# Layer 2 of a routed kernel: rows gathered by quarters in groups of four, transposed in blocks by VectorE, with four output buffers

## The chip, the cores and the metric

The kernel runs on one core of a Trainium2 chip. The metric is the device time of one execution in microseconds (us); three runs of the kernel before gave 972.41, 974.34 and 975.12, median 974.34. In the profile PE is TensorE (PEld its weight loads), DVE is VectorE, ACT is ScalarE, POOL is GpSimd, SP is the queue that issues plain DMAs. Indirect DMAs (gathers and scatters of rows) are issued by POOL, in program order with its other work.

## The reference

An attention layer is followed by two mixture-of-experts layers of 8 experts over 2304 rows of 512 numbers. Layer 1 picks one expert per row, layer 2 two. The part that matters here is layer 2:

```
logits = x @ w_gate; noisy = logits + log1p(exp(x @ w_noise)) * noise
top2 = two largest of noisy per row; top2_w = softmax over these two
for e in range(8):
    for k in range(2):
        mask = top2[:, k] == e
        h = max(x[mask] @ w1[e], 0)            # 512 -> 1024
        out[mask] += top2_w[mask, k] * (h @ w2[e])   # 1024 -> 512
```

All of it is float32. The kernel splits each factor of a product into a high and a low part and adds three products, high·high, low·high and high·low.

## The kernel before

Attention and the routing of layer 1 are laid out by a planner with costs and due times (`Tasks.order`); layers 1 and 2 are written in the order in which they are issued (`full`, `pair`, `layer2`). Each engine runs its own instructions in that order.

At the end of each unit of layer 1, `x1_out` (L881) writes 2 × 128 finished rows to a DRAM buffer `xd` (520 numbers per row: 512 of data and 8 of noise). Rows of it that no unit writes are cleared during attention by DMAs on SP's queue, spread by the planner over the attention chunks (`M.later`, five DMAs to a chunk).

Layer 2 takes the 8 experts one after the other, 640 row slots (5 tiles of 128) each. The first two tiles of expert 0 are layer 1's last ones and are worked off while the routing of the last rows runs (`route2`); `slot_tables` then turns the routing into row numbers for the gathers (`l2g`) and the scatters (`l2s`). In the loop over experts e there are two stages:

- First products: `mm1` for 8 blocks f, in two halves of 304 columns each, 12 matmuls a half (L721 to L723) into a PSUM bank; ACT takes the high part (`hh`, L724), DVE the low part (`hl`, L726). There are two such banks. ACT and DVE also split the weights w2 (`split_w`, L696 and L697).
- Second products: `mm2` for 5 tiles, each in two half-tiles q of 12 matmuls of 512 columns (L731 to L733). Between half-tiles a list `todo` is worked off, with the splits of the next expert's w1 (`split_w1`, L700 and L701) and its 5 row tiles (`xsplit`): four transposes of 128×128 on TensorE against an identity (L711), then ACT's high part from PSUM (L712) and DVE's low part (L713). After each tile `l2_out` scales it on ACT into one of two output buffers (`os`, L973) and POOL scatters it with an addition into the output (L974). A scatter waits until the one before has landed.

The five gathers for expert e+1 (`l2_gather`, L704: 128 rows of 520 numbers each) are issued in one burst at the start of expert e, on POOL behind the scatters of expert e−1. If an expert has more than 640 rows, `overflow` does the rest; with these inputs it does not run.

Of the kernel before, what the change touches and what calls it, by code (L numbers as in the profile page):

```python
# [307 lines left out]
class Moe:  # L308
    def __init__(s, ctx, tc, ident, consts, areas):
# [3 lines left out]
        s.dram=ctx.enter_context(tc.tile_pool(name='dram',bufs=1,space=bass.MemoryType.DRAM))  # L313
        s.xd=s.dram.tile([N+SLOTS,XW],FT,name='xd')
# [35 lines left out]
    def blocks(s, nc, c, areas):  # L350
# [7 lines left out]
        s.w1r=V(T(K0,0,4096,'w1r'),KD); s.w2r=V(T(K0,4096,4096,'w2r'),KF); s.os=cut(K0,8192,512,'os',2)  # L358
# [6 lines left out]
        s.wb1=[V(T(HL,o,2048,'wb1%d'%o),2) for o in (2048,7168)]; s.wb2=V(T(W2,4096,4096,'wb2'),KF)  # L365
        s.x1=V(T(X1,0,2*XW,'x1'),2); s.ol2=V(T(OL,0,512,'ol2',FR),4); s.gs=cut(G,0,XW,'gs',GB); s.gn_=s.on_=0
# [603 lines left out]
    def l2_out(s, wk, y, tb, c, out):  # L970
# [3 lines left out]
        nc.gpsimd.indirect_dma_start(out=out,out_offset=bass.IndirectOffsetOnAxis(ap=si[:,c:c+1],axis=0),in_=o,in_offset=None,compute_op=OP.add)  # L974
    def l2_gather(s, wk, tb, c, ts=range(T2)):
        return [s.gather(s.xd[:],tb[0][:,c+t:c+t+1]) for t in ts]
    def layer2(s, w1, w2, out):
# [33 lines left out]
        V.tensor_copy(ov[:,NOV:],ue[:,E-1:E])  # L1011
        for e in range(E):
            nxt=e+1<E
            if nxt:
                if e: s.load_w(s.w1r,w1,E+e+1)
                g=s.l2_gather(wk,tb,(e+1)*TS)
            for f in range(KF):
# [4 lines left out]
                else: s.mm1(ps,f,EARLY,C2-EARLY)  # L1022
            if nxt and e: s.load_w(s.w2r,w2,E+e+1)
            ts=range(T2) if e else range(NE,T2)
            todo=[(lambda f=f:s.split_w1(f,nc.vector)) for f in range(KF)]
            for t in range(T2): todo.insert(2*t+1,lambda t=t:s.xsplit(ps,g[t],t*128))
            n=-(-len(todo)//(2*len(ts)-1))
            for t in ts:
                for q in range(2):
                    y=s.mm2(ps,t*128,range(4*q,4*q+4),y if q else None)  # L1030
                    if nxt:
                        for _ in range(n):
                            if todo: todo.pop(0)()
                s.l2_out(wk,y,tb,e*TS+t,out)
# [54 lines left out]
def build(tc, q, k, v, mz, beta, ids, mbias, wg, w1, w2, wcat, noise, out):  # L1089
    nc = tc.nc  # L1090
    with ExitStack() as ctx:
# [24 lines left out]
        M.later = [Q.add(100 * (5 + j // 5), SP, 1000, f, [A.sunk[4 + j // 5]]) for j, f in enumerate(dma)]  # L1116
# [51 lines left out]
```

## Time and profile before

| | us |
|---|---|
| median of 3 runs | 974.34 (972.41 to 975.12) |
| the profiled execution | 980.08 |
| its span, first to last instruction | 978.4 |
| TensorE busy | 941.9 (96%) |
| VectorE, ScalarE, GpSimd busy | 554.9, 487.9, 349.1 |
| mean granted clock of TensorE | 0.989 |

The page gives busy time by engine, the span in slices, the chain that ended last and the costliest groups of instructions. Attention fills the span up to about 190 us, layer 1 up to about 500, layer 2 the rest. Busy time of TensorE rests on modelled ends of matmuls, so lengths below are taken from start to start where that is possible.

### The profile page before, as it was taken

The numbers are of one execution on the slowest core, as the hardware profiler recorded it, in microseconds if no ns is written. First come the engines' busy times: TensorE is split into PE (matmuls) and PEld (weight loads), VectorE is DVE, ScalarE is ACT, GpSimd is POOL, SyncE is SP. The second block draws the span as 40 slices with busy tenths as digits, with TensorE's granted clock in tenths as the row PEclk, the third lists the DMA queues.
The fourth block names the chain that finished last, engine by engine and source line by source line (L and its number), as shares of the span: only waits on it lengthen the run. The fifth ranks groups of instructions, "written<-read, shape, count | busy, mean of one in ns | idle before, by whom it ended". The sixth has DMA issues, their size and how long they took to land. (4 is left out here: it accounts for less than half of the span.)

```text
span 978.4 us, 18585 instructions
## 1 busy us (share of the span) xinstructions
PE 941.9 (96%) x6849; PEld 828.6 (85%) x6849; DVE 554.9 (57%) x1697; ACT 487.9 (50%) x1141; POOL 349.1 (36%) x418
## 2 busy tenths in 40 slices
PE   7999999998999999999998999999999999999994
PEld 5888888878876888888887998898989889898983
DVE  8777777788765777777774344242443424253310
ACT  6887878775433565555552344333343434343320
POOL 5222231234552667776765130312213030221111
PEclk9999999999999999999999999999999999999997
DMA  8345856261595665555655163545346364435112
GB/s 212 102 111 178 268 193 207 78 225 59 192 313 188 214 215 195 191 193 202 216 198 159 38 172 97 128 132 129 77 113 168 97 137 130 122 78 119 22 23 35
DMA packets 83857, 144.98 MB, mean 148 GB/s; under 512 B 14497, under 2 KB 32929, under 8 KB 83745
## 3 DMA queue, kind: packets, MB, share of 16 engines
q1 hardware_dynamic: 73184, 117.10, 36.4%
q0 software_dynamic: 10560, 26.47, 13.6%
q8 instruction: 60, 0.98, 0.4%
q14 instruction: 53, 0.43, 0.1%
HBM read 111.65 MB, written 31.97 MB: 147 GB/s over the span
## 5 line engine op out<-in xcount | busy, mean ns | idle before, releaser
L721 PE MATMUL b<-xh,w1h 128*128 128x304 f32 (+3 forms) x800 | 240.5, 301 | 4.2 <-DVE hl L726 1.4
L722 PE MATMUL b<-xl,w1h 128*128 128x304 f32 (+3 forms) x800 | 237.7, 297 | 0.6 <-DVEq L791 0.3
L723 PE MATMUL b<-xh,w1l 128*128 128x304 f32 (+3 forms) x800 | 237.0, 296 | 0.0
L726 DVE SCALAR_TENSOR_TENSOR hl<-b,hh 128x304 fp32r<-128x304 f32 (+3 forms) x200 | 91.1, 455 | 209.3 <-ACT hh L724 198.1
L731 PE MATMUL b<-w2h,hh 128*128 128x512 f32 x464 | 187.8, 405 | 0.0
L974 POOL DMA_INDIRECT out_dram<-os,l2s x40 | 62.8, 1571 | 333.6 <-ACT os L973 256.9
L733 PE MATMUL b<-w2h,hl 128*128 128x512 f32 x464 | 181.6, 391 | 0.0
L732 PE MATMUL b<-w2l,hh 128*128 128x512 f32 x464 | 181.0, 390 | 0.0
L724 ACT ACTIVATE hh<-b 128x304 fp32r<-128x304 f32 (+3 forms) x200 | 81.8, 409 | 172.8 <-PE b L723 166.8
L721 PEld LDWEIGHTS b<-xh,w1h 128*128 128x128 f32 x800 | 152.6, 191 | 11.5 <-DVE hl L726 6.2
L722 PEld LDWEIGHTS b<-xl,w1h 128*128 128x128 f32 x800 | 152.6, 191 | 1.6 <-DVEq L791 0.5
L723 PEld LDWEIGHTS b<-xh,w1l 128*128 128x128 f32 x800 | 152.5, 191 | 0.0
L733 PEld LDWEIGHTS b<-w2h,hl 128*128 128x128 f32 x464 | 87.1, 188 | 19.4
L732 PEld LDWEIGHTS b<-w2l,hh 128*128 128x128 f32 x464 | 87.5, 188 | 15.5
L731 PEld LDWEIGHTS b<-w2h,hh 128*128 128x128 f32 x464 | 87.2, 188 | 15.4
L151 ACT ACTIVATE p<-sm,l 128x128 f32<-128x128 f32 (+4 forms) x144 | 84.1, 592 | 17.5 <-DVE l L147 17.5
L701 DVE TENSOR_TENSOR w1l<-w1r,w1h 128x512 fp32r<-128x512 f32 x86 | 71.5, 841 | 18.6 <-ACT w1h L700 18.3
L713 DVE TENSOR_TENSOR xl<-b,xh 128x512 fp32r<-128x512 f32 x56 | 38.6, 689 | 71.3 <-ACT xh L712 71.2
L696 ACT CAST w2h<-w2r 128x512 fp32r<-128x512 f32 x128 | 78.5, 613 | 0.0
L712 ACT CAST xh<-b 128x512 fp32r<-128x512 f32 x56 | 32.9, 587 | 87.4 <-PE b L711 87.4
L700 ACT CAST w1h<-w1r 128x512 fp32r<-128x512 f32 x128 | 74.8, 620 | 0.0
L973 ACT ACTIVATE os<-b,l2w 128x512 f32<-128x512 f32 x40 | 27.7, 691 | 94.1 <-PE b L733 47.9
(460 smaller groups left out, 1504.7 us busy)
## 6 DMA issues: line engine op xcount, KB each, us to landing
w1r<-in_w_dram SPq DMA_DIRECT2D x18, 2048.0 KB, 9.0
w2r<-in_w_dram SPq DMA_DIRECT2D x18, 2048.0 KB, 9.1
xd<-gs SPq DMA_DIRECT2D x24, 260.0 KB, 4.1
xd<-x SPq DMA_DIRECT2D x10, 520.0 KB, 10.8
out_dram<-gs SPq DMA_DIRECT2D x19, 256.0 KB, 3.8
k<-in_k_dram SPq DMA_DIRECT2D x16, 256.0 KB, 4.9
q<-in_q_dram SPq DMA_DIRECT2D x16, 256.0 KB, 3.3
v<-in_v_dram SPq DMA_DIRECT2D x16, 256.0 KB, 3.9
```

The lines of the kernel that those rows point to most:

```text
L151: s.nc.scalar.activation(s.P[b,i,u][:,lh*n:lh*n+n],s.SM[b,i,u][:,lh*n:lh*n+n],AF.Exp,scale=-1.0,bias=L[:,0,c:c+1],accum_out=L[:,1,c:c+1])
L696: nc.scalar.copy(hi[c],raw[:,c])
L700: nc.scalar.copy(s.w1h[:,:,fs],s.w1r[:,:,fs])
L701: eng.tensor_sub(s.w1l[:,:,fs],s.w1r[:,:,fs],s.w1h[:,:,fs].bitcast(FT))
L721: nc.tensor.matmul(h[:,:n],s.w1h[:,k,fs],s.xh[:,k,cs],start=k==0,stop=False)
L722: nc.tensor.matmul(h[:,:n],s.w1h[:,k,fs],s.xl[:,k,cs],start=False,stop=False)
L723: nc.tensor.matmul(h[:,:n],s.w1l[:,k,fs],s.xh[:,k,cs],start=False,stop=k==KD-1)
L724: def mm1_a(s, h, f, c0, n): s.nc.scalar.activation(s.hh[:,f,c0:c0+n],h[:,:n],AF.Relu)
L726: cs=slice(c0,c0+n); s.nc.vector.scalar_tensor_tensor(s.hl[:,f,cs],h[:,:n],0.0,s.hh[:,f,cs].bitcast(FT),op0=OP.max,op1=OP.subtract)
L731: nc.tensor.matmul(y,s.hh[:,f,cs],s.w2h[f],start=f==0,stop=False)
L732: nc.tensor.matmul(y,s.hh[:,f,cs],s.w2l[f],start=False,stop=False)
L733: nc.tensor.matmul(y,s.hl[:,f,cs],s.w2h[f],start=False,stop=f==KF-1)
```

## The change

Each unit's rows are written twice, to `xd` and, without the noise, to a second buffer `xq` in which every row is four rows of 128 numbers. Clearing covers `xq` too, with seven DMAs to a chunk. In layer 2's loop a tile is fetched by four gathers of 128 rows of 128 numbers: gather i brings, for slots 32i to 32i+31, quarter g of the row into partitions 32g to 32g+31 (`quarter_gather`, with the row numbers `gq4` from `quarter_tables`, made by four small products with a selection matrix from `quarter_sel`). One VectorE instruction then transposes the tile in blocks of 32×32 (`bsplit`), which puts feature 4P+j into partition P; w1 is loaded in the same order of features (`by='(p c)'`). ACT and DVE split from SBUF. Tiles 3 and 4 of expert 1 are gathered as whole rows and transposed on TensorE, by every fourth column (`xsplit` with `fourth`). The groups are spread over the loop by a table `plan`: tiles 1, 2 and 3 of the next expert after f = 1, 4 and 7 of the first products, tile 4 and tile 0 of the one after it between second products. Ahead of most groups GpSimd copies one column of a tensor that VectorE writes (`pace`), which holds the group back until then. The output buffers become four.

```diff
+        s.xq=s.dram.tile([4*SLOTS,D//4],FT,name='xq')
...
+        s.gq=cut(G,0,D,'gq',GB); s.xt_=[V(t,KD) for t in cut(X1,0,D,'xtq',2)]; s.xn=0; s.sel4=V(T(K1,8192,512,'sel4',FR),4); s.sel4f=V(T(K1,8704,512,'sel4f'),4)
...
-    def load_w(s, raw, w, e, eng=None):
-        src=(w[bass.ds(e,1)] if not isinstance(e,int) else w[e:e+1]).rearrange('o (c p) f -> p (o c) f',p=128)
+    def load_w(s, raw, w, e, eng=None, by='(c p)'):
+        src=(w[bass.ds(e,1)] if not isinstance(e,int) else w[e:e+1]).rearrange('o %s f -> p (o c) f'%by,p=128)
...
     def o(s):
-        s.on_+=1; return s.os[s.on_%2]
-    def xsplit(s, ps, g, c0):
+        s.on_+=1; return s.os[s.on_%len(s.os)]
+    def bsplit(s, g, c0):
+        nc=s.nc; x=s.xt_[s.xn%2]; s.xn+=1
+        nc.vector.transpose(x.rearrange('p j (s t) -> p s j t',s=4),g.rearrange('p (s d j) -> p s j d',s=4,j=KD))
+        nc.scalar.copy(s.xh[:,:,c0:c0+128],x)
+        nc.vector.tensor_sub(s.xl[:,:,c0:c0+128],x,s.xh[:,:,c0:c0+128].bitcast(FT))
+    def xsplit(s, ps, g, c0, fourth=False):
         nc=s.nc
         tp=ps.tile([128,KD,128],FT,name='tp')
-        for k in range(KD): nc.tensor.transpose(tp[:,k],g[:,k*128:(k+1)*128],s.ident)
+        for k in range(KD): nc.tensor.transpose(tp[:,k],g[:,k:D:4] if fourth else g[:,k*128:(k+1)*128],s.ident)
         nc.scalar.copy(s.xh[:,:,c0:c0+128],tp)
         nc.vector.tensor_sub(s.xl[:,:,c0:c0+128],tp,s.xh[:,:,c0:c0+128].bitcast(FT))
         return tp
...
     def x1_out(s, c, n):
-        d=s.xd[N:].rearrange('(c p) d -> p c d',p=128)
-        s.nc.sync.dma_start(d[:,c:c+n] if isinstance(c,int) else d[:,bass.ds(c,n)],s.x1[:,:n])
+        d=s.xd[N:].rearrange('(c p) d -> p c d',p=128); dq=s.xq[:].rearrange('(c p q) d -> p c (q d)',p=128,q=4)
+        for d,w in ((d,XW),(dq,D)): s.nc.sync.dma_start(d[:,c:c+n] if isinstance(c,int) else d[:,bass.ds(c,n)],s.x1[:,:n,:w])
...
+    def quarter_sel(s):
+        G=s.nc.gpsimd; f=s.sel4f
+        G.memset(f,0.0)
+        G.affine_select(f.rearrange('p s (g t) -> p s g t',g=4),f.rearrange('p s (g t) -> p s g t',g=4),pattern=[[-32,4],[0,4],[-1,32]],compare_op=OP.not_equal,fill=1.0,base=0,channel_multiplier=1)
+        G.tensor_copy(s.sel4,f)
+        for g in range(4): G.memset(s.qn[32*g:32*g+32],float(g))
...
+    def quarter_tables(s, part):
+        nc=s.nc; V=nc.vector
+        if part==0:
+            s.mq=s.c.tile([128,NC2],FR,name='mq'); s.gq4=s.c.tile([128,4,NC2],I32,name='gq4'); s.gq1=s.c.tile([128,NC2],I32,name='gq1')
+            V.tensor_copy(s.mq,s.M2[:,0])
+            V.tensor_scalar(s.gq1,s.M2[:,0],float(S0),0.0,op0=OP.add,op1=OP.max)
+            return
+        f=s.c.tile([128,4,NC2],FT,name='fq')
+        p=s.ps.tile([128,512],FT,name='sm')
+        for i in range(4): nc.tensor.matmul(p[:,i*NC2:(i+1)*NC2],s.sel4[:,i],s.mq,start=True,stop=True)
+        V.tensor_scalar(f,p[:,:4*NC2].rearrange('p (s c) -> p s c',s=4),float(S0),0.0,op0=OP.add,op1=OP.max)
+        V.tensor_scalar(s.gq4,f,4.0,s.qn[:,0:1],op0=OP.mult,op1=OP.add)
+    def quarter_gather(s, e, t, behind=None, whole=False):
+        c=e*TS+t; G=s.nc.gpsimd
+        if behind is not None: G.tensor_copy(s.pace,behind.bitcast(FT))
+        if whole: G.indirect_dma_start(out=s.gq[t],out_offset=None,in_=s.xq[:].rearrange('(c q) d -> c (q d)',q=4),in_offset=bass.IndirectOffsetOnAxis(ap=s.gq1[:,c:c+1],axis=0))
+        else:
+            for i in range(4): G.indirect_dma_start(out=s.gq[t][:,i*128:(i+1)*128],out_offset=None,in_=s.xq[:],in_offset=bass.IndirectOffsetOnAxis(ap=s.gq4[:,i,c:c+1],axis=0))
...
-        s.load_w(s.w1r,w1,E+1)
+        s.load_w(s.w1r,w1,E+1,by='(p c)')
         s.chain=s.route2(wk,ps,NF+NP2,2); s.hold=0
         for f in range(KF):
             s.mm1(ps,f,DEAD,EARLY-DEAD)
             if f==1: s.behind()
             if f in LSLOT2: s.logits(wk,ps,1+LSLOT2.index(f))
+            if f==5: s.quarter_sel()
             s.split_w(s.w2r,s.w2h,s.w2l,f,nc.vector if f<3 else nc.gpsimd)
             if f>LSLOT2[2]: s.pump(f,GATE2,PUMP2)
...
-                    ge=s.l2_gather(wk,tb,0,range(NE,T2))
+                    ge=s.l2_gather(wk,tb,0,range(NE,T2)); s.quarter_tables(0)
                 elif t==NE-1 and q==2: s.xsplit(ps,ge[0],NE*128)
             if t==NE-1: s.xsplit(ps,ge[1],(NE+1)*128)
             s.l2_out(wk,y,tb,t,out)
+        s.quarter_tables(1)
...
+        plan={}
+        for e in range(E):
+            p=plan[e]=dict(f={},i={})
+            n=lambda w,at,d,t: d<E and p[w].setdefault(at,[]).append((d,t))
+            if e:
+                for t,f in ((1,1),(2,4),(3,7)): n('f',f,e+1,t)
+                n('i',3,e+1,4); n('i',7,e+2,0)
+            else:
+                n('f',3,1,1); n('f',6,1,2); n('i',0,1,3); n('i',0,1,4); n('i',4,2,0)
+        s.quarter_gather(1,0)
         for e in range(E):
             nxt=e+1<E
-            if nxt:
-                if e: s.load_w(s.w1r,w1,E+e+1)
-                g=s.l2_gather(wk,tb,(e+1)*TS)
+            if nxt and e: s.load_w(s.w1r,w1,E+e+1,by='(p c)')
             for f in range(KF):
                 if e:
                     s.mm1(ps,f,DEAD,CH)
                     s.split_w(s.w2r,s.w2h,s.w2l,f)
                     s.mm1(ps,f,DEAD+CH,CH)
                 else: s.mm1(ps,f,EARLY,C2-EARLY)
+                for d,t in plan[e]['f'].get(f,()): s.quarter_gather(d,t,s.hl[:,f,C2-1:C2])
             if nxt and e: s.load_w(s.w2r,w2,E+e+1)
-            ts=range(T2) if e else range(NE,T2)
+            ts=range(T2) if e else range(NE,T2); whole=(3,4) if not e else ()
             todo=[(lambda f=f:s.split_w1(f,nc.vector)) for f in range(KF)]
-            for t in range(T2): todo.insert(2*t+1,lambda t=t:s.xsplit(ps,g[t],t*128))
+            for t in range(T2): todo.insert(2*t+2 if t<4 else len(todo),lambda t=t:s.xsplit(ps,s.gq[t],t*128,True) if t in whole else s.bsplit(s.gq[t],t*128))
             n=-(-len(todo)//(2*len(ts)-1))
             for t in ts:
                 for q in range(2):
                     y=s.mm2(ps,t*128,range(4*q,4*q+4),y if q else None)
+                    i=2*(t-ts[0])+q
                     if nxt:
                         for _ in range(n):
                             if todo: todo.pop(0)()
+                    for k,(d,t_) in enumerate(plan[e]['i'].get(i,())): s.quarter_gather(d,t_,None if k else s.w1l[:,0,min(i+1,7)*128:min(i+1,7)*128+1],d==1)
                 s.l2_out(wk,y,tb,e*TS+t,out)
...
             dma.append(lambda r=r: nc.sync.dma_start(M.xd[r:r + 128], zt))
-        M.later = [Q.add(100 * (5 + j // 5), SP, 1000, f, [A.sunk[4 + j // 5]]) for j, f in enumerate(dma)]
+            dma.append(lambda r=r: nc.sync.dma_start(M.xq[4 * (r - N):4 * (r - N) + 512].rearrange('(p q) d -> p (q d)', q=4), zt[:, :D]))
+        M.later = [Q.add(100 * (5 + j // 7), SP, 1000, f, [A.sunk[4 + j // 7]]) for j, f in enumerate(dma)]
```

On TensorE, in the second products of expert 1, after the fourth block f of the first tile; b is a PSUM bank, w2h and w2l the split weights, hh and hl the split hidden values, gs a gathered tile. Before:

```order
L731 MATMUL b_159<-w2h_72,hh_87 128x512
L732 MATMUL b_159<-w2l_80,hh_87 128x512
L733 MATMUL b_159<-w2h_72,hl_88 128x512
L711 MATMUL b_160<-ident,gs_99 128x128 x4
L731 MATMUL b_159<-w2h_73,hh_87 128x512
```

And in the changed kernel at the same place:

```order
L739 MATMUL b_170<-w2h_74,hh_89 128x512
L740 MATMUL b_170<-w2l_82,hh_89 128x512
L741 MATMUL b_170<-w2h_74,hl_90 128x512
L739 MATMUL b_170<-w2h_75,hh_89 128x512
L740 MATMUL b_170<-w2l_83,hh_89 128x512
```

The four transposes between the blocks are gone; the products stand next to each other. This holds for all five tiles of experts 2 to 7 and for three of expert 1's.

On POOL, from the start of expert 1's first products; gs and gq are gathered tiles, os the output buffers. Before:

```order
L704 DMA gs_99<-xd,l2g 128x520
L704 DMA gs_100<-xd,l2g 128x520
L704 DMA gs_101<-xd,l2g 128x520
L704 DMA gs_97<-xd,l2g 128x520
L704 DMA gs_98<-xd,l2g 128x520
L974 DMA out_dram<-os_61,l2s 2432x512
L974 DMA out_dram<-os_62,l2s 2432x512
```

And now, over the whole of expert 1's two stages up to its eighth half-tile:

```order
L1006 COPY pace<-hl_90 128x1
L1009 DMA gq_98<-xq,gq_8405 128x128 x4
L1006 COPY pace<-hl_90 128x1
L1009 DMA gq_99<-xq,gq_8405 128x128 x4
L1006 COPY pace<-hl_90 128x1
L1009 DMA gq_100<-xq,gq_8405 128x128 x4
L982 DMA out_dram<-os_63,l2s 2432x512
L1006 COPY pace<-w1l 128x1
L1009 DMA gq_101<-xq,gq_8405 128x128 x4
L982 DMA out_dram<-os_64,l2s 2432x512
L982 DMA out_dram<-os_61,l2s 2432x512
L1006 COPY pace<-w1l 128x1
```

Five gathers in one piece have become groups of four quarter gathers, each behind a copy that waits for DVE, and two groups stand among the scatters.

On POOL, while expert 0's early tiles are worked off; w2l are low parts of w2, wh belongs to the routing. Before:

```order
L697 TENSOR_TENSOR w2l_81<-w2r,w2h_73 128x512
L697 TENSOR_TENSOR w2l_82<-w2r,w2h_74 128x512
L697 TENSOR_TENSOR w2l_83<-w2r,w2h_75 128x512
L697 TENSOR_TENSOR w2l_84<-w2r,w2h_76 128x512
L939 CAST wh<-w__8271 128x4
```

And now:

```order
L699 TENSOR_TENSOR w2l_83<-w2r,w2h_75 128x512
L986 MEMSET sel4f 128x512
L987 AFFINE_SELECT sel4f<-sel4f 128x512
L988 CAST sel_104<-sel4f 128x512
L989 MEMSET qn 32x1 x4
L699 TENSOR_TENSOR w2l_84<-w2r,w2h_76 128x512
L699 TENSOR_TENSOR w2l_85<-w2r,w2h_77 128x512
L699 TENSOR_TENSOR w2l_86<-w2r,w2h_78 128x512
L947 CAST wh<-w__8335 128x4
```

The selection matrix is made between the splits of blocks f = 4 and f = 5, ahead of the routing's copies.

## Rows read from the trace of the kernel before

**Rows 1.** Page, part 1: busy time, share of the span, instructions
```profile
PE 941.9 (96%) x6849; PEld 828.6 (85%) x6849; DVE 554.9 (57%) x1697; ACT 487.9 (50%) x1141; POOL 349.1 (36%) x418
```
**Rows 2.** Windows, layer 2: length, busy (count) of PE, PEld, DVE, ACT, POOL, PEclk, DMA
```profile
551.20:569.90 18.70, 18.70 (x93) 15.51 (x93) 8.99 (x14) 8.66 (x16) 3.20 (x2) 1.00 0.16 20
596.94:626.60 29.66, 29.66 (x142) 24.48 (x141) 9.30 (x15) 10.02 (x18) 5.08 (x4) 1.00 0.60 167
626.60:653.27 26.67, 26.67 (x193) 26.66 (x192) 12.48 (x23) 11.10 (x24) 7.92 (x7) 1.00 0.35 72
682.94:710.44 27.50, 26.94 (x194) 26.69 (x192) 12.47 (x23) 11.10 (x24) 7.94 (x7) 1.00 0.34 70
936.93:964.20 27.27, 27.27 (x122) 22.35 (x120) 0.68 (x2) 3.18 (x5) 6.20 (x4) 1.00 0.30 38
```
**Rows 3.** Windows, sum line over stages from 569.90, 682.94, 740.10, 797.08, 853.64
```profile
sum 135.72, PE 134.68 PEld 133.44 DVE 62.26 ACT 55.50 POOL 38.06; mean PE 26.94 PEld 26.69 DVE 12.45 ACT 11.10 POOL 7.61
```
**Rows 4.** Timeline, ACT and PE near 698: start, us, engine, line, operation [idle <-releaser]
```profile
697.69 0.42 ACT L724 ACTIVATE hh<-b 128x304 fp32r<-128x304 f32 x1 [1.94 <-PE b L723]
698.68 0.41 PE L721 MATMUL b<-xh,w1h 128*128 128x304 f32 x1 [0.56 <-DVE hl L726]
```
**Rows 5.** Timeline, PE, second products of expert 2, 653 to 660
```profile
653.27 0.39 PE L731 MATMUL b<-w2h,hh 128*128 128x512 f32 x1
...
656.02 0.60 PE L711 MATMUL b<-ident,gs 128*128 128x128 f32 x4
...
659.23 0.60 PE L711 MATMUL b<-ident,gs 128*128 128x128 f32 x4
```
**Rows 6.** Lines, DVE, from 500: group, count, busy us, mean ns, idle before
```profile
L697 DVE TENSOR_TENSOR w2l<-w2r,w2h 128x512 fp32r<-128x512 f32 x59 | 40.9, 693 | 3.5 <-ACT w2h L696 1.7
...
L904 DVE TENSOR_TENSOR qn<-b,nz 128x16 f32<-128x16 f32 x1 | 0.2, 165 | 0.0
```
**Rows 7.** Timeline, POOL, 688 to 693: scatter and first gathers of a burst
```profile
688.75 1.55 POOL L974 DMA_INDIRECT out_dram<-os,l2s  x1 [4.11 <-ACT hh L724]
690.61 1.02 POOL L704 DMA_INDIRECT gs<-xd,l2g  x1 [0.30 <-issue]
691.93 0.98 POOL L704 DMA_INDIRECT gs<-xd,l2g  x1 [0.30 <-issue]
```
**Rows 8.** Timeline, POOL, DVE, PE, start of layer 2
```profile
514.14 1.28 POOL L697 TENSOR_TENSOR w2l<-w2r,w2h 128x512 fp32r<-128x512 f32 x1 [0.43 <-ACT w2h L696]
516.92 1.28 POOL L697 TENSOR_TENSOR w2l<-w2r,w2h 128x512 fp32r<-128x512 f32 x1 [1.50 <-ACT w2h L696]
...
519.69 0.96 DVE L947 TENSOR_TENSOR rrm<-b,val 128x768 fp32r<-128x768 f32 x1 [0.60 <-POOL val L939]
...
522.33 0.99 POOL L704 DMA_INDIRECT gs<-xd,l2g  x1 [2.55 <-DVE l2w L964]
...
528.13 0.41 PE L711 MATMUL b<-ident,gs 128*128 128x128 f32 x2 [1.21 <-issue]
```
**Rows 9.** Lines, POOL, whole span: fills, select, arithmetic pass
```profile
L123 POOL TENSOR_SCALAR ph<-q 128x512 f32<-128x512 f32 x16 | 23.7, 1486 | 74.3 <-ACT oc L186 32.5 <-PE b L175 15.4 <-ACT p L151 12.0
...
L1101 POOL MEMSET gs<- 128x520 f32 x1 | 0.5, 540 | 0.0
...
L325 POOL TENSOR_SCALAR_AFFINE_SELECT tri<-tri 128x128 f32<-128x128 f32 x1 | 0.3, 292 | 0.1
```
**Rows 10.** Timeline, DVE, expert 0's first product f = 6
```profile
549.84 0.56 DVE L726 SCALAR_TENSOR_TENSOR hl<-b,hh 128x384 fp32r<-128x384 f32 x1 [1.52 <-ACT hh L724]
```
**Rows 11.** Windows, the first products after the still stand
```profile
534.00:538.00 4.00, 4.00 (x16) 4.00 (x15) 0.56 (x1) 0.49 (x1) 3.09 (x4) 0.57 0.90 167
```
**Rows 12.** Waits of PE in attention; timeline, SP, 94 to 96; timeline, PE, 116
```profile
PE b L139 <- DMA q<-in_q_dram: 6.8, 2, 5.8
...
94.46 0.55 SPq L114 DMA_DIRECT2D q<-in_q_dram  x1
...
116.18 1.14 PE L139 MATMUL b<-k,q 64*128 64x256 f32 x10
```

More of the change, by code (lines that the diff above doesn't have):

```diff
@@ L357, in blocks @@
         K0,K1,X,HL,W2,G,X1,OL=range(8)
-        s.w1r=V(T(K0,0,4096,'w1r'),KD); s.w2r=V(T(K0,4096,4096,'w2r'),KF); s.os=cut(K0,8192,512,'os',2)
+        s.w1r=V(T(K0,0,4096,'w1r'),KD); s.w2r=V(T(K0,4096,4096,'w2r'),KF); s.os=cut(K0,8192,512,'os',2)+[T(OL,0,512,'os2'),T(K1,8704,512,'os3')]
         s.w1h=V(T(K1,0,4096,'w1h',FR),KD); s.w1l=V(T(K1,4096,4096,'w1l',FR),KD); s.yt=V(T(K1,8192,1024,'yt'),KD); s.rr=c.tile([128,4,256],FR,name='rrm')
@@ L739, in state @@
         nc=s.nc; c=s.c
-        s.run=c.tile([128,E],FT,name='run'); nc.gpsimd.memset(s.run,float(DEAD))
+        s.qn=c.tile([128,1],FT,name='qn'); s.pace=c.tile([128,1],FT,name='pace'); s.run=c.tile([128,E],FT,name='run'); nc.gpsimd.memset(s.run,float(DEAD))
         s.M2=c.tile([128,4,NC2],FT,name='M2'); nc.gpsimd.memset(s.M2,0.0)
@@ L1078, in overflow @@
                 e=nc.values_load(ov[0:1,o:o+1],engines=[ET.SP],min_val=0,max_val=E-1)
-                s.load_w(s.w1r,w1,e+E); s.load_w(s.w2r,w2,e+E)
+                s.load_w(s.w1r,w1,e+E,by='(p c)'); s.load_w(s.w2r,w2,e+E)
                 for ff in range(KF): s.split_w1(ff,nc.vector)
-                for t,g in enumerate(s.l2_gather(wk,tb,o*T2)): s.xsplit(ps,g,t*128)
+                for t,g in enumerate(s.l2_gather(wk,tb,o*T2)): s.xsplit(ps,g,t*128,True)
                 for ff in range(KF):
```

## The prediction

> **What bounds the kernel now.** I read the engine shares first. TensorE is busy for 941.9 of 978.4 us [rows 1], so time is gained only where TensorE's own list of instructions gets shorter, and lost only where TensorE is made to wait. Next I cut layer 2 at its stages [rows 2]. Each expert has a stage of 192 first products (columns 304 wide) and a stage of 120 second products (512 wide) with 20 transposes among them. In the second-product stage TensorE is busy for 29.66 of 29.66 us, VectorE for 9.30 and ScalarE for 10.02: the transposes sit on the full engine, and the engine that is to take them is two thirds idle. The last expert has no successor and so no transposes, and its stage takes 27.27 us. Third, the five first-product stages in which row gathers run for the next expert (first and last of them at 569.90 and 853.64) come to 135.72 us, 2.37 us more than five times the 26.67 us of an undisturbed one [rows 2, 3]. There ScalarE's copy of a product starts late, for a semaphore of TensorE that came late, and TensorE then waits for the bank [rows 4]. The burst there begins at 690.61, so its fifth gather runs from 695.7 to 696.7 [rows 7] and ScalarE's copy starts at 697.69, which should have followed a product that ended by 696.5; the burst before the stage at 626.60 did not do it.
>
> **The change part by part, against the profiled execution: 980.08 us, a span of 978.4 and 1.7 around it.** That execution is 5.7 us slower than the median of the runs, 974.34. I work out a difference and take it off the median.
>
> 1. *Transposes removed.* In the main loop of layer 2 TensorE's list has 35 groups of four transposes before and 2 after, so 33 go. From the second products to the next group takes 2.75 us without one (653.27 to 656.02) and 3.21 us with one (656.02 to 659.23) [rows 5], so a group costs 0.46 us. As a check, (29.66 − 27.27) / 5 = 0.48. All of it is on the path. 33 × 0.46 = 15.2 us; with 0.48 it is 15.8.
>
> [...]
>
> 2. *What VectorE takes on.* Per expert five block transposes of 128×512, and subtractions whose first operand is now in SBUF. No row shows the transpose. From below: a two-operand pass over as many elements, 693 ns [rows 6]. From above: sixteen short operations, one for each 32 columns, at 165 ns, 2.6 us. I take 0.7, the row with the same elements. Even at 2.6 the stage has 5 × 2.6 more on top of 9.30, which is 22.3 of about 27.3 us. It costs nothing, because it lies beside the products. The subtraction from SBUF is of the same form as that row. ScalarE makes the same copies, from SBUF.
>
> 3. *Gathers by quarters.* Four gathers of 128 rows for one. A gather holds GpSimd for 1.02 us plus 0.30 to the next, a scatter 1.55 [rows 7]. Per expert 20 × 1.32 + 5 × 1.85 = 35.7 us, of a period of 26.67 + 27.3 = 54.0. Before, it was 5 × 1.32 + 9.3 = 15.9. So it fits, and the spare 18.3 us is the cover: it is used up at 2.2 us a gather. The price of a quarter gather lies between nothing and a scatter's 1.55 + 0.30; same rows, same index count, so I take the gather row. Each group waits for a VectorE result first. Queued behind it on GpSimd stand the scatters, for which ScalarE waits through the output buffers: two would hold it up, four are enough for a delay of 5.3 us a group. The group of tile 4 waits for a split of w1 that ScalarE reaches after the first output tile (5.5 us into the stage) and about 4.5 us of copies; with its 5.3 us it is issued by 15.3 of 27.3 us, and its split is needed after the end, so TensorE does not wait.
>
> 4. *Bursts.* No burst of five is left. The first four gathers of each burst before show no late semaphore, so I take the 2.4 us of [rows 3] as regained; the other end is in the first rival.
>
> 5. *Start of layer 2.* Before, GpSimd runs the splits of w2 with gaps of 0.43 and 1.50 us, and after the last one rows that routing waits for [rows 8]. VectorE's product L947 waits 0.60 us for them, and from it hangs the first gather (522.33), for which TensorE stands still until 528.13. New among the splits: a fill of 128×512 (0.54 for 520 columns), a select (0.29 for 128 columns, so 0.3 to 1.2), a cast (between that fill's 0.54 and the 1.49 of an arithmetic pass) and four tiny fills of about 0.1 [rows 9]. That is 1.8 to 3.6, I take 2.4; less the gaps of 1.93, 0.5 us late (0 to 1.7). The four selecting products and two short VectorE operations ahead of the last subtraction add 0.3. Together +0.8 (0 to 2.0).
>
> 6. *Expert 1's whole gathers.* They stand on GpSimd behind the quarters that wait for first-product f = 6, whose VectorE half ends at 550.40 [rows 10]. Four gathers later it is 555.7; TensorE comes to the transpose of tile 3 after three half-tiles of 12 products, 551.20 + 3 × 2.73 = 559.4. From a gather's issue to its use the start of layer 2 took 5.8 us (522.33 to 528.13) [rows 8], with DMA traffic beside it: 561.5, a wait of 2.1 us. With the 1.0 us that the instruction itself takes there is none. DMA is nearly idle here, 0.16 [rows 2]; I take the middle, +1.0 (0 to 2.1). [...]
>
> 7. *Second copy of the rows in DRAM, and its clearing.* Some 24 fills of 256 KB and ten of 512 KB more on SP's queue. In attention TensorE waits for a load 6.8 us in all, 5.8 of it one wait at the start [rows 12]; the load that moves most, by nine or ten fills of about 0.7 us and a wait, is issued at 94.46, some 22 us ahead of its scores at 116.18. I take 0 (0 to 1.5). Weights by 16 KB runs: 0.
>
> Sum: −15.2 − 2.4 + 0.8 + 1.0 = −15.8 us, so 964.3 in such a profiled execution and **958.5 us** as median.
>
> **Rivals.**
>
> *Groups of four delay the semaphore too.* For: a burst of five cost 2.37 / 6 = 0.4 us each, and why is not in the trace. Against: it came with the fifth. There are now 20 groups beside first products: 20 × 0.4 = 8.0 back, total −7.8, 966.5 us. At the largest single loss, 27.50 − 26.67 = 0.83 [rows 2], 16.6 come back: +0.8, no change.
>
> *GpSimd becomes the bound.* If a quarter gather takes more than 2.2 us, the last tile is late in every expert. At 2.6 us an expert takes 20 × 2.6 + 9.3 = 61.3 us instead of 54.0; six experts lose 44 us, less 15.8: 1002 us, slower. From 2.35 us on (2.6 us per expert) the change loses. For: gathers of other sizes aren't in the trace. Against: five gathers of 128 rows go out 1.32 us apart without waiting for landing [rows 7].
>
> *The stage doesn't shrink.* VectorE would have to need over 3.5 us per block transpose ((27.3 − 9.3) / 5): no change, 974. Against: even sixteen pieces are 2.6.
>
> **How the numbers follow.** Forecast 0.74, its own range 955 to 962 (−18.2 − 1 us of spread to −12); late semaphores at mean size 0.13, at full size 0.04; GpSimd as bound 0.05; no shrinkage 0.02; other mishaps of small size 0.02. A change of 0.3% (2.9 us) is what can be told from none. Faster 0.88, same 0.05, slower 0.07. The range 955 to 967.5 takes in the forecast and the first rival's mean.
>
> **What would show it.** Second-product stages near 27.4 us with no transposes in them; first-product stages at 26.7; groups of four gathers of about 5.3 us on GpSimd, some 10 us apart; block transposes well under 3 us; TensorE's start of expert 0's products about 0.8 us later; one wait of TensorE at expert 1's tile 3. Wrong would be: gathers of over 2 us, ScalarE's copies late beside each group, or stages that keep 29.7 us.

## The result, and the profile after

The changed kernel takes 960.01 us (median of 4 runs, 958.26 to 960.46), the kernel before 974.65 beside it (4 runs): ratio 0.9851, 95% interval 0.9831 to 0.9871, so 12.6 to 16.5 us less. 958.5 was predicted, in a range of 955 to 967.5. Measured again beside the experiments it gave 0.9855 (0.9837 to 0.9873). The profiled execution is its shortest, 958.26 us with a span of 956.5. Against the profiled execution of before that is 21.8 us, 7 more than the medians differ. Some 3.4 of these 7 are clock: before, TensorE's granted clock was 0.50 in three stretches of 3.4 us ahead of its end (from 206.6, 223.7 and 534.3, the last in [rows 11]), after in one (from 263.8), and such a stretch costs 1.7 us, an estimate (half of 3.4). Another 2.4 are the bursts of [rows 3]. So stages are compared below, and not spans.

Part 1 of the page after, busy time and share of the span, answers to [rows 1]:

```profile
PE 923.1 (97%) x6721; PEld 814.1 (85%) x6721; DVE 589.4 (62%) x1734; ACT 490.2 (51%) x1141; POOL 470.0 (49%) x557
```

TensorE has 128 records less and stays the bound; GpSimd took on 121 us. The stages of layer 2, in windows of the kernel after (columns as in [rows 2]): expert 0's second products, then first and second products of experts 1 and 2.

```profile
547.02:565.56 18.54, 17.64 (x81) 14.42 (x81) 11.84 (x17) 8.76 (x16) 12.03 (x12) 1.00 0.47 118
565.56:592.23 26.67, 26.67 (x193) 26.66 (x192) 12.40 (x23) 11.10 (x24) 12.12 (x14) 1.00 0.33 87
592.23:619.46 27.23, 27.23 (x123) 22.53 (x121) 14.22 (x20) 10.34 (x18) 13.28 (x13) 1.00 0.64 193
619.46:646.12 26.66, 26.66 (x193) 26.66 (x192) 12.54 (x23) 11.10 (x24) 18.02 (x18) 1.00 0.35 60
646.12:673.35 27.23, 27.23 (x122) 22.53 (x121) 14.13 (x20) 10.34 (x18) 12.97 (x13) 1.00 0.66 194
```

Six second-product stages went from 29.66 to 27.23, 14.6 us in all, and all seven first-product stages take 26.67. Expert 0's stage lost three groups of transposes and yet went only from 18.70 to 18.54: TensorE is busy for 17.64 of it, the rest is a wait.

The new operations, in the groups of instructions (the block transpose on VectorE in layer 2, the quarter gathers on the page), and the last tile of an expert in the timelines of GpSimd and VectorE (start, us, engine, line, operation, idle before):

```profile
L713 DVE STREAM_TRANSPOSE xtq<-gq 128x512 f32<-128x512 f32 x33 | 35.6, 1078 | 45.4 <-DMA gq<-xq,gq 45.4
```

```profile
L1009 POOL DMA_INDIRECT gq<-xq,gq x132 | 136.4, 1034 | 39.1 <-issue 36.9
```

```profile
608.59 0.95 POOL L1009 DMA_INDIRECT gq<-xq,gq  x1 [0.30 <-issue]
```

```profile
616.35 1.08 DVE L713 STREAM_TRANSPOSE xtq<-gq 128x512 f32<-128x512 f32 x1 [8.28 <-DMA gq<-xq,gq]
618.18 0.69 DVE L715 TENSOR_TENSOR xl<-xtq,xh 128x512 fp32r<-128x512 f32 x1 [0.74 <-ACT xh L714]
```

A quarter gather holds GpSimd as long as a whole one (1.03 us; [rows 7] has 1.02). The last gather of tile 4 ends at 609.5 and its rows are there only at 616.3, 6.8 us later. The load of w1 (2 MB, issued at 608.09) runs beside it; between 570 and 592, without a load, a gather's rows were there 2.5 to 3.1 us after its start. The split of tile 4 ends at 618.87; the products that read it start 1.67 us after 619.46, so 2.3 us were left.

The start of layer 2 and expert 1's tile 3 (GpSimd, then TensorE), answering to [rows 8]:

```profile
509.18 0.53 POOL L986 MEMSET sel4f<- 128x512 f32 x1
509.78 0.73 POOL L987 TENSOR_SCALAR_AFFINE_SELECT sel4f<-sel4f 128x512 f32<-128x512 f32 x1
510.58 0.61 POOL L988 CAST sel<-sel4f 128x512 fp32r<-128x512 f32 x1
511.13 0.47 POOL L989 MEMSET qn<- 32x1 f32 x4
...
519.48 0.99 POOL L706 DMA_INDIRECT gs<-xd,l2g  x1 [2.55 <-DVE l2w L972]
```

```profile
525.35 0.63 PE L719 MATMUL b<-ident,gs 128*128 128x128 f32 x4 [1.32 <-issue]
...
556.28 0.72 PE L719 MATMUL b<-ident,gq 128*128 128x128 f32 x4 [0.90 <-DMA gq<-xq,gq]
```

From the first early second product (512.56; before 515.78) to TensorE's first transpose it is 12.79 us now and 12.35 before: 0.44 later. At 556.28 TensorE stands 0.90 us for the rows of tile 3.

### The profile page after: what moved, and what is told of

Its sections match the earlier page's. It is cut to its first block, busy times and chain, and to the rows that moved or that the text cites. A ratio compares the mean times of both kernels' runs of the same rounds, so it can differ in the third digit from the quotient of the medians.

```text
span 956.5 us, 18482 instructions
## 1 busy us (share of the span) xinstructions
PE 923.1 (97%) x6721; PEld 814.1 (85%) x6721; DVE 589.4 (62%) x1734; ACT 490.2 (51%) x1141; POOL 470.0 (49%) x557
## 3 DMA queue, kind: packets, MB, share of 16 engines
q0 software_dynamic: 12144, 26.33, 14.1%
## 5 line engine op out<-in xcount | busy, mean ns | idle before, releaser
L739 PE MATMUL b<-w2h,hh 128*128 128x512 f32 x464 | 184.7, 398 | 0.0
L1009 POOL DMA_INDIRECT gq<-xq,gq x132 | 136.4, 1034 | 39.1 <-issue 36.9
L982 POOL DMA_INDIRECT out_dram<-os,l2s x40 | 66.8, 1669 | 130.7 <-ACT os L981 55.1
L740 PEld LDWEIGHTS b<-w2l,hh 128*128 128x128 f32 x464 | 87.5, 189 | 16.4
L739 PEld LDWEIGHTS b<-w2h,hh 128*128 128x128 f32 x464 | 87.5, 189 | 16.4
L699 POOL TENSOR_TENSOR w2l<-w2r,w2h 128x512 fp32r<-128x512 f32 x45 | 59.0, 1313 | 31.0 <-ACT w2h L698 23.1
L147 DVE CUSTOM_DVE_ANT_0 sm<-b,mask 128x128 f32<-128x128 f32 (+4 forms) x144 | 63.0, 479 | 12.1 <-PE b L139 7.8
```

The source lines that it names most:

```text
L739: nc.tensor.matmul(y,s.hh[:,f,cs],s.w2h[f],start=f==0,stop=False)
L740: nc.tensor.matmul(y,s.hh[:,f,cs],s.w2l[f],start=False,stop=False)
L1009: for i in range(4): G.indirect_dma_start(out=s.gq[t][:,i*128:(i+1)*128],out_offset=None,in_=s.xq[:],in_offset=bass.IndirectOffsetOnAxis(a ...
```

## The experiments

The runs fall into sets. Each set ran on one chip and is compared with the kernel before on that chip: E1 to E4 on chip A (before: 976.66 us), E5 to E8 on chip B (973.95), E9 to E11 on chip C (978.07), E12 on chip C again (975.89). For the first measurement, above, no chip is on record. It turned out that one and the same order of instructions can cost nothing in one set and 7 to 20 us a stage in another (E10, E12). In the code cuts `...` stands for lines of the edit that are left out.

**E1, transposes back on TensorE.** The changed kernel with

```diff
-def quarter_gather(s, e, t, behind=None, whole=False):
+def quarter_gather(s, e, t, behind=None, whole=True):
-whole=(3,4) if not e else ()
+whole=range(T2)
...
```

> The changed kernel, with every tile gathered as whole rows (one gather where there were four, at the same places of the plan) and transposed on TensorE. Theory (term 1 of the prediction: the transposes on TensorE are the gain): second-product stages of experts 1 to 6 go from 27.2 back to about 29.6 us, expert 0's by 1.4 us, while first-product stages stay at 26.67 since no burst comes back; 33 x 0.46 to 0.49 = 15.2 to 16 us on 960.0, so about 975, or 973 if counted from the kernel before (974.65 less 2.4 for bursts, plus 0.4 for the later start). Rival (the gain comes from the spacing of the gathers or from four output buffers): stays within 3 us of 960.

978.75 us, ratio 1.0017 (1.0006 to 1.0029): the gain is gone, and everything else that the change adds costs 1.7 us. First and second products of expert 1, in windows:

```profile
571.98:598.65 26.67, 26.67 (x193) 26.66 (x192) 12.39 (x23) 11.10 (x24) 3.98 (x5) 1.00 0.31 82
598.65:628.44 29.79, 29.79 (x142) 24.96 (x141) 9.09 (x15) 10.06 (x18) 9.11 (x9) 1.00 0.66 190
```

(29.79 − 27.23) / 5 = 0.51 us a group. The ratios put the transposes at 1.0017 − 0.9855, some 16 us; the rival falls. The run takes the transposes back together with the quarter gathers and VectorE's block transposes, as one package, and the two ratios come from chips A and B.

**E2, one row of gathers.** All gathers for expert e + 1 at the start of expert e, without waits:

```diff
+if nxt:
+    for t in range(0 if e else 1,T2): s.quarter_gather(e+1,t,None,not e and t>2)
-for d,t in plan[e]['f'].get(f,()): s.quarter_gather(d,t,s.hl[:,f,C2-1:C2])
...
```

> The changed kernel, with all gathers for the next expert issued in one row at the start of its first products (20 quarter gathers, 25 us of GpSimd; expert 1's rest likewise), no waits ahead of groups. Theory A (a row of gathers longer than four makes TensorE's semaphore late, whatever the size of a row): every first-product stage with a burst loses at least the 0.4 us that the bursts of five cost, so 962.4, and up to 16 late ones a stage at 0.4, 6 x 6.4 = 38 us: 998. Theory B (spacing isn't needed; late semaphores came from rows of 2 KB or from something else): first-product stages stay at 26.67 and the time at 960.

1077.97 us, ratio 1.1038: 100 us slower. A first-product stage in a window, and ScalarE in it (timeline):

```profile
580.56:625.62 45.06, 31.55 (x193) 30.68 (x192) 12.28 (x23) 10.99 (x24) 20.82 (x21) 0.85 0.25 72
```

```profile
596.15 0.61 ACT L698 CAST w2h<-w2r 128x512 fp32r<-128x512 f32 x1
599.99 0.42 ACT L732 ACTIVATE hh<-b 128x304 fp32r<-128x304 f32 x1 [3.23 <-PE b L731]
608.55 0.42 ACT L732 ACTIVATE hh<-b 128x304 fp32r<-128x304 f32 x1 [8.14 <-remote]
```

It is the pattern of [rows 4], with waits four times as long: there 1.94 us, in this stage 8.14, for a signal of TensorE whose last product of that bank had started at 602.60. The row of gathers had begun at 588.64. Theory A's mechanism is right in kind for this set, but its size is 16 to 18 us a stage and not 0.4 to 6.4.

**E3, the kernel before with its five gathers spread.**

```diff
-g=s.l2_gather(wk,tb,(e+1)*TS)
+g=s.l2_gather(wk,tb,(e+1)*TS,[0])
...
+if nxt and f in (1,3,5,7):
+    nc.gpsimd.tensor_copy(s.pace,s.hl[:,f,C2-1:C2].bitcast(FT)); g+=s.l2_gather(wk,tb,(e+1)*TS,[(f+1)//2])
```

> The kernel before, with its five gathers spread: the first at the expert's start, the others behind VectorE's half of first product f = 1, 3, 5 and 7. Theory (term 4): the five disturbed first-product stages go back to 26.67 us, 2.4 us in all: 972.3. Rival (the 2.4 us came by chance in the profiled execution, or from something beside the gathers): no change, 974.65, and stages above 27 still in the trace.

976.15 us, ratio 0.9999 (0.9990 to 1.0009). One of its first-product stages in a window, the third, which took 27.50 before [rows 2]:

```profile
679.86:706.53 26.67, 26.67 (x193) 26.66 (x192) 12.46 (x23) 11.12 (x24) 7.36 (x9) 1.00 0.30 63
```

All of them take 26.67, and the time shows at most 1 us of it: what one profiled execution lost to bursts, 2.4 us, is not what the medians lose. E4, which keeps the bursts on the same chip, lost 1.4 us in its profiled execution, 27.41 the longest stage (window):

```profile
680.92:708.33 27.41, 26.96 (x194) 26.70 (x193) 12.46 (x23) 11.10 (x24) 7.94 (x7) 1.00 0.32 70
```

So the loss comes back from one execution to another, in a changing size.

**E4, the kernel before with the second copy**, written and cleared as in the change, and the same again in the list of clearings:

```diff
-s.nc.sync.dma_start(d[:,c:c+n] if isinstance(c,int) else d[:,bass.ds(c,n)],s.x1[:,:n])
+for d,w in ((d,XW),(dq,D)): s.nc.sync.dma_start(d[:,c:c+n] if isinstance(c,int) else d[:,bass.ds(c,n)],s.x1[:,:n,:w])
...
```

> The kernel before, with the second copy of the rows written and cleared as in the changed kernel, and never read. Term 7 of the prediction: 0, at most 1.5 us, so 974.65 to 976.2. Rival (the copy is what ate the missing part of the gain, since the stages account for about 17 us and the medians for 14.6): about 977.

977.65 us, ratio 1.0018 (1.0006 to 1.0031): 1.8 us, 0.6 to 3.0. TensorE's timeline has a wait in attention where it had none:

```profile
112.06 0.35 PE L175 MATMUL b<-mzs,ph 128*128 128x130 f32 x1 [0.51 <-DMA mzs<-in_mz_dram]
```

SP's fills are now ahead of other loads of attention than the one I had looked at; this row is 0.51 us of the price. Where the rest is lost the runs don't show, and in the profiles of the changed kernel itself (the first and E5) TensorE doesn't wait for this load at all.

**E5, the changed kernel again.**

> The changed kernel again, as the base of the next ones and for a narrower interval. Sum of what the runs so far show: transposes and what hangs on them 16.2 us less (its own ratio against the one with TensorE's transposes), second copy 1.8 more, later start 0.4 more, bursts 0 to 1 less: 14 to 15 us below the kernel before, ratio 0.985. Had the first measurement been lucky, the ratio would rise to 0.987 or more.

959.47 us, ratio 0.9855: the first measurement was not lucky.

**E6, the row broken.** E2 with a copy of a ready column on GpSimd ahead of each group:

```diff
-s.quarter_gather(e+1,t,None,not e and t>2)
+s.quarter_gather(e+1,t,s.qn[:,0:1],not e and t>2)
```

> The kernel of the row of 20 gathers (1078 us) with one copy of a ready 128x1 column on GpSimd ahead of each group of four; nothing waits, the row stays 26 us long. Theory A (a row that nothing breaks holds back the other engines' semaphores; any other instruction of GpSimd ends it): first-product stages return to 26.7 and the time to about 960. Theory B (what counts is how many gathers go out in a time, and only the 10 us between groups help): stages stay at 40 us or more and the time above 1050.

960.29 us, ratio 0.9859 (0.9839 to 0.9880), and first-product stages like this one (window):

```profile
621.48:648.15 26.67, 26.67 (x193) 26.66 (x192) 12.46 (x23) 11.12 (x24) 15.56 (x18) 1.00 0.31 55
```

That looked like proof of theory A. E9, E10 and E12 undid it, and the row without copies (E2) was never run on chip B. One thing stands: with the whole gathers issued earlier here, expert 0's second products take 17.40 us, so without the wait of tile 3 the three groups are worth 18.70 − 17.40 = 1.3.

**E7, two output buffers.**

```diff
-s.os=cut(K0,8192,512,'os',2)+[T(OL,0,512,'os2'),T(K1,8704,512,'os3')]
+s.os=cut(K0,8192,512,'os',2)
```

> The changed kernel with two output buffers instead of four. Term 3 of the prediction (two would hold ScalarE up): in the trace the scatters of tiles 2, 1 and so on go out 7.7 to 13.9 us after their tile's end, so ScalarE's scaling of tile 4 waits 3 to 5 us at the start of each first-product stage and TensorE behind it; six experts at 2 to 5 us: 972 to 990. Rival (ScalarE and the banks have room for the wait): no change, 960.

981.13 us, ratio 1.0081 (1.0059 to 1.0102), 21.7 us over E5. ScalarE's timeline at the start of expert 2's first products:

```profile
623.98 0.69 ACT L981 ACTIVATE os<-b,l2w 128x512 f32<-128x512 f32 x1 [4.90 <-DMA out_dram<-os,l2s]
624.57 0.42 ACT L732 ACTIVATE hh<-b 128x304 fp32r<-128x304 f32 x1
```

The scaling of tile 4 waits 4.90 us until a scatter has landed, and the copy of the next expert's product queues behind it, so TensorE has no bank: it waits 2.12 us at 625.55. Five first-product stages take 30.5 to 31.4 us, 21.1 more in all.

**E8, three moves**, with the clearing of `xq` put behind the other clearing in the list `dma`.

```diff
-if f==5: s.quarter_sel()
+if f==2: s.quarter_sel()
-n('f',3,1,1); n('f',6,1,2); n('i',0,1,3); n('i',0,1,4); n('i',4,2,0)
+n('f',3,1,1); n('f',5,1,3); n('f',5,1,4); n('f',6,1,2); n('i',4,2,0)
...
-M.later = [Q.add(100 * (5 + j // 7), SP, 1000, f, [A.sunk[4 + j // 7]]) for j, f in enumerate(dma)]
+M.later = [Q.add(100 * (5 + j // 5), SP, 1000, f, [A.sunk[4 + j // 5]]) for j, f in enumerate(dma)]
```

> The changed kernel with three moves: the selection matrix is made at f = 2, where GpSimd is idle, instead of f = 5 (0.4 us, term 5); expert 1's two whole gathers go out behind f = 5, ahead of tile 2's quarters, instead of behind the first half-tile (0.9 us of TensorE's wait, term 6); the clearing of the second copy comes after the other clearing, five DMAs to a chunk as before (term 7: 1.0 to 1.8 us). Theory: 2.3 to 3 us less, 957.5, and the wait at expert 1's tile 3 gone. Rival (none of these was on the path, or another wait takes their place): within 1 us of 960.

965.13 us, ratio 0.9909 (0.9892 to 0.9926), 5.7 slower than E5. The two moves in layer 2 did what was expected; early second products and expert 0's second products:

```profile
519.88:536.43 16.55, 13.78 (x71) 10.91 (x69) 7.60 (x24) 3.79 (x7) 7.45 (x11) 1.00 0.63 192
553.89:571.28 17.39, 17.39 (x81) 14.49 (x81) 11.86 (x17) 8.75 (x16) 10.27 (x10) 1.00 0.41 101
```

16.55 us is the length of before (E5 has 17.12, the selection matrix's 0.5), and 17.39 is a stage without the wait (E5 has 18.81): 2.0 us gained, by stages. More was lost ahead, by a step that I had not followed: the planner lets layer 1's first row gathers wait for all of the clearing (`[fs[0]]+s.later`), and the later list pushes them back. SP's last clearing, GpSimd's gather, TensorE's wait and the granted clock behind it:

```profile
216.91 0.43 SPq L1166 DMA_DIRECT2D xq<-gs  x1
```

```profile
220.41 1.68 POOL L706 DMA_INDIRECT gs<-xd,gidx  x1 [3.90 <-issue]
```

```profile
224.48 1.11 PE L555 MATMUL b<-ident,gs 128*128 128x128 f32 x4 [4.10 <-DMA gs<-xd,gidx]
```

```profile
223.13:233.37 10.24, 7.19 (x38) 6.12 (x39) 4.69 (x14) 3.37 (x8) 7.63 (x12) 0.50 0.61 194
```

In the changed kernel the first of these gathers is issued at 208.1. Here TensorE waits 4.10 us, and its granted clock is 0.50 for 10.2 us, where the changed kernel has 1.00 in the same window: by an estimate some 5 us more (half of 10.2).

**E9, the broken row with all of expert 1 by quarters**, and the selection matrix at f = 2: E6 with

```diff
-s.quarter_gather(e+1,t,s.qn[:,0:1],not e and t>2)
+s.quarter_gather(e+1,t,s.qn[:,0:1])
-whole=(3,4) if not e else ()
+whole=()
```

> The kernel with the broken row of gathers (960.3), with all of expert 1's tiles by quarters and VectorE as well, and the selection matrix made at f = 2. Theory: layer 2 starts 0.4 us earlier (term 5; seen in the run with the early moves), expert 0's second products lose their last two groups of transposes and every wait, so about 72 x 0.227 = 16.4 us instead of 18.6 in the changed kernel: 2.5 us less than 959.5, so 957. Rival (tile 4 of expert 1 lands too late for the first products behind it, since 20 gathers fill GpSimd until about 560): 1 to 4 us of wait there, 958 to 961.

1080.94 us, ratio 1.1049 (1.1018 to 1.1081). Neither theory had that: the first-product stages of experts 1 to 6 take 43.7 to 46.3 us, much as in E2 (42.7 to 45.1), though their order on GpSimd is E6's. The time says nothing of the two moves. By stages, the early second products take 16.49 us, as in E8, and expert 0's second products 17.19 and not 16.4.

**E10, rows of eight**: E6 with the copy ahead of every second group only.

```diff
-s.quarter_gather(e+1,t,s.qn[:,0:1],not e and t>2)
+s.quarter_gather(e+1,t,s.qn[:,0:1] if t%2==0 or not e else None,not e and t>2)
```

> The kernel with the broken row, with a copy on GpSimd only ahead of every second group, so rows of eight, eight and four gathers for experts 2 to 7 (expert 1 as it was). Theory (TensorE's signals come late from the fifth or sixth gather of an unbroken row on, and go through when the row ends): 1 to 4 us lost for each row of eight, 2 rows x 6 experts: 972 to 1008. Rival (only much longer rows hurt): stages at 26.7, 960.

1077.51 us, ratio 1.1020 (1.1002 to 1.1038). Up to expert 1's first products this program is E6's, instruction by instruction on every engine. Yet expert 0's first products, E6 first:

```profile
531.17:550.19 19.02, 18.59 (x96) 18.33 (x97) 5.32 (x13) 3.45 (x7) 15.32 (x19) 0.91 0.27 60
```

```profile
534.36:560.65 26.29, 20.74 (x96) 19.85 (x97) 5.32 (x13) 3.44 (x7) 15.56 (x19) 0.87 0.26 60
```

What differs is not the program. The chips do, B there and C here, but so do the sets: the runs don't separate the chip from the session in which a program ran.

**E11, slow gathers.** Behind every quarter gather:

```diff
...
+[G.memset(s.spare,0.0) for _ in range(6)]
```

> The changed kernel with six fills of 128x128 on GpSimd after every quarter gather, some 1.2 us, as if a gather took 2.5 us. The prediction's rival (GpSimd becomes the bound from 2.2 us a gather): 20 x 2.5 + 5 x 1.85 = 59.3 us of GpSimd against 53.9 of products, six experts lose 5.4 us each: about 990; with the pace copies (5 x 0.9) 10 us each and 1019. Other theory (the buffers and the order leave no room even before that): more than 1030. If the cover were larger than worked out: below 970.

1074.70 us, ratio 1.1007 (1.0979 to 1.1034): of the three, only the other theory allows that. GpSimd's timeline, and an expert's two stages in windows:

```profile
647.43 0.99 POOL L1010 DMA_INDIRECT gq<-xq,gq  x1 [0.16 <-issue]
648.42 1.54 POOL L1010 MEMSET spare<- 128x128 f32 x6
650.12 0.96 POOL L1010 DMA_INDIRECT gq<-xq,gq  x1 [0.16 <-issue]
...
655.89 1.88 POOL L982 DMA_INDIRECT out_dram<-os,l2s  x1 [0.58 <-ACT w2h L698]
661.92 1.59 POOL L982 DMA_INDIRECT out_dram<-os,l2s  x1 [4.15 <-ACT hh L732]
```

```profile
633.78:666.08 32.30, 28.76 (x194) 28.28 (x192) 14.28 (x25) 12.08 (x26) 20.28 (x48) 0.95 0.32 49
666.08:708.15 42.07, 31.93 (x122) 25.36 (x121) 12.56 (x18) 8.91 (x16) 35.06 (x106) 0.84 0.42 130
```

A gather takes 2.7 us (647.43 to 650.12), and an expert 74.4 us (expert 2) where the prediction's formula gives 20 × 2.7 + 9.3 = 63.3. The formula counts GpSimd's work and not its waits; behind a scatter GpSimd stands some 4 us until that one has landed (at 661.92 the row names ScalarE, which had long been done; E12 has such a wait at 862.17, 3.78 us, in which the row names the scatter before). The cover is smaller than worked out: if the 11 us that the formula lacks (74.4 − 63.3) are taken as such waits, it ends at (53.9 − 9.3 − 11) / 20 = 1.7 us a gather, not 2.2, an estimate from this run. The change has 1.33. The run is on chip C, where rows of gathers make signals late; here that has little part, for in this expert's two stages ScalarE's copies wait 2.2 us for TensorE at most.

**E12, three ways side by side**: no copies for experts 1 and 2, copies for 3 and 4, the changed kernel's plan for 5 and 6.

```diff
+if 1<=e<=4:
+    for t in range(T2): s.quarter_gather(e+1,t,s.qn[:,0:1] if e>2 else None)
-    for t,f in ((1,1),(2,4),(3,7)): n('f',f,e+1,t)
-    n('i',3,e+1,4); n('i',7,e+2,0)
+    if e>4:
+        for t,f in ((1,1),(2,4),(3,7)): n('f',f,e+1,t)
+        n('i',3,e+1,4)
+    if e>3: n('i',7,e+2,0)
...
```

> One kernel with three ways to gather side by side, each for two experts: an unbroken row of 20 quarter gathers at the start of experts 1 and 2, the row broken by a copy ahead of each group for experts 3 and 4, the changed kernel's spaced groups for experts 5 and 6. The broken row was harmless in one set of runs (960.3) and cost 17 us an expert in another set with the same order of instructions, so either the copies help, or it is not the program that decides. Theory A (the copies break the row): first-product stages of 1 and 2 take 43 to 45 us, those of 3 to 6 26.7; some 993 us. Theory C (the chip or the session that the set ran on decides): 1 to 4 all take 43 to 45 us, about 1027, or all take 26.7 us, about 960. Theory D (spaced groups suffer too where rows do): 5 and 6 over 27 us as well.

1037.09 us, ratio 1.0616 (1.0594 to 1.0638). First-product stages of experts 1 to 6:

```profile
569.36:612.49 43.13, 30.78 (x193) 29.90 (x192) 12.41 (x23) 11.11 (x24) 20.89 (x21) 0.80 0.24 64
639.72:684.20 44.48, 31.84 (x193) 30.84 (x192) 12.36 (x23) 11.02 (x24) 21.87 (x22) 0.77 0.19 42
711.43:757.28 45.85, 30.37 (x193) 29.50 (x192) 12.33 (x23) 11.01 (x24) 22.34 (x27) 0.81 0.18 41
784.51:829.92 45.41, 30.14 (x193) 29.40 (x192) 12.37 (x23) 11.02 (x24) 22.26 (x27) 0.85 0.19 41
857.15:883.82 26.67, 26.67 (x194) 26.67 (x192) 12.46 (x23) 11.12 (x24) 11.18 (x12) 1.00 0.22 40
911.04:940.62 29.58, 27.24 (x194) 26.73 (x192) 12.54 (x23) 11.01 (x24) 17.73 (x18) 1.00 0.31 54
```

Copies or none, the rows cost 16.5 to 19.2 us an expert: theory A falls, and of theory C (the chip or the session) the first form holds. Spaced groups cost nothing for expert 5 and 2.9 us for expert 6, so D holds in part. What sets these two apart stands in GpSimd's timeline of expert 6:

```profile
925.50 0.78 POOL L1006 COPY pace<-hl 128x1 f32<-128x1 f32 x1
...
930.35 0.94 POOL L1009 DMA_INDIRECT gq<-xq,gq  x1 [0.31 <-issue]
931.30 0.20 POOL L1006 COPY pace<-hl 128x1 f32<-128x1 f32 x1
```

The scatters ahead held the group of f = 1 up to 925.5, and that of f = 4 follows it without a gap; in expert 5 the two start 10 us apart (865.08 and 875.08).

## Why the prediction was right, and where it was off

The sum was −15.8 us, the time says −14.6 (−12.6 to −16.5) and −14.1 (−12.4 to −15.9). By its steps:

1. *Transposes*, −15.2: right, a little more. Six stages give 14.6 and expert 0's 1.3 (E6): −15.9. By the trace a group costs 0.49 us.
2. *VectorE's block transposes*, 0: right, though they take 1.08 us and not 0.7; VectorE is busy for 14.2 of 27.2 us. E1, which keeps the transposes on TensorE, is some 16 us slower.
3. *Quarter gathers*, 0: right on time, with 1.03 us a gather and four output buffers that are needed (E7, +21.7). Two parts were off: the groups are not 10 us apart everywhere (the pairs below), and the cover is smaller (E11).
4. *Bursts*, −2.4: mis-sized. The stages did come back to 26.67, but E3, which does this part alone, moves the time by 0.1 us, 1 at most. The step took the loss of one execution, and of one 5.7 us above the median, for the median's.
5. *Start of layer 2*, +0.8: 0.44 measured, all of it the work of `quarter_sel`. What was put down for `quarter_tables`, 0.3, is not there: from the first transpose to the first products it is 4.20 us before and after.
6. *Expert 1's tile 3*, +1.0: right, 0.9 in the profile and 1.1 to 1.4 by stages (18.54 and E5's 18.81 against 17.40).
7. *Second copy*, 0: too low. E4 has 1.8 (0.6 to 3.0). I had asked only whether the loads of q are moved past the fills; E4's TensorE lost 0.51 us at another load, and where the rest went is open.

With these the sum is −15.9 − 0.1 + 0.4 + 1.3 + 1.8 = −12.5, 2 us short of the measured 14.6, within its uncertainties: 4 and 7 erred in one direction, 5 a little in the other. So the mechanism was right, the transposes carry the gain, but that the forecast of 958.5 lies only 1.5 us from 960.01 is in part luck: terms 4 and 7 alone were off by 2.3 and 1.8 us.

The first rival, groups that delay TensorE's signal, was given 0.17 and priced at 0.4 to 0.83 us a group, and didn't come in the profiles of the changed kernel. It did come in E12, on chip C: where two groups follow each other, ScalarE waits up to 3.27 us for TensorE (at 934.97; 0.72 or 1.25 is usual), and the stage takes 2.9 us more. The changed kernel has such a pair in five experts, the first in GpSimd's timeline of the kernel after:

```profile
633.36 0.78 POOL L1006 COPY pace<-hl 128x1 f32<-128x1 f32 x1
...
639.11 0.60 POOL L1006 COPY pace<-hl 128x1 f32<-128x1 f32 x1
```

5 × 2.9 = 14.5 us would take back the whole gain under the conditions of E12. That is an estimate from one stage: the changed kernel has no run on chip C, and none that is known to be on A, so its gain is shown for chip B and for the chip of the first measurement. E8 shows what is left to gain: 2.0 us, by stages, by the two moves in layer 2 without the third. That version was not run on its own; E9 holds the first of them, with another cure for the second, but ran on chip C.

## What to carry to other kernels

Move work off the full engine onto one that the same stage leaves idle, and size the gain by comparing a stage that has the work with one that hasn't: 0.46 to 0.48 us a group was read before, and 0.49 to 0.51 came out. A stall whose cause the trace doesn't show, in one execution, is worth a range and not a term. Before you compare two versions of an order of gathers, run them in the same set on the same chip, or side by side in one kernel.

## What the runs showed of the hardware

- In E2 on chip A and in E9, E10 and E12 on chip C, ScalarE waits for TensorE beside a row of quarter gathers on GpSimd, some 1.25 us apart, up to 8.1 us in the stage of E2 above and 12.4 in E12, where 0.7 or 1.3 is usual. It begins after five to nine gathers, ends some 3 us after the row and costs 16 to 20 us a row of 20 in E2, E9 and E12 (stages of 42.7 to 46.3 us against 26.67). In E6 on chip B such a row, with copies, costs nothing (26.67). Whether the chip decides or the session, and by what, is open.
- In all these runs, and in E4, E11 and the profile of before, the answers on DMA have no landing time for any gather in the first-product stages; on B, and in the profile after, most or all have one. It is not the chip alone: in E3, on chip A like E2 and E4, one of the four in each stage has one. Issues in a first-product stage, E12's expert 6, the kernel after and E3:

```profile
gq<-xq,gq POOLq DMA_INDIRECT x12
```

```profile
gq<-xq,gq POOLq DMA_INDIRECT x12, 2.7
```

```profile
gs<-xd,l2g POOLq DMA_INDIRECT x4, 3.3
```

  So landing times are missing in every execution in which signals come late, but also where none does: E12's expert 5 has no landing time either, and its stage takes 26.67 us. What the missing landing times have to do with the delay, the runs don't show; all of them were recorded, so whether the recording has a part in the delay, and in the times, was not tried.
- In the kernel after, the rows of a quarter gather are there 2.5 to 3.1 us after its start without a load beside it (570 to 592), and 7.6 us after it beside a 2 MB load (608.59).
